# Row-maximum products of a pooled attention kernel moved onto 64 contraction rows each

## Chip, cores and metric

The kernel runs on one core of one Trainium2 chip, in one launch. The metric is the device time in microseconds; the time of before is the median of three runs.

## What is computed

```python
B, H, S, D = 4, 8, 1152, 64
q_pool = q.reshape(B, H, S // 2, 2, D).mean(axis=3)
scores = scale * np.matmul(q_pool, k.transpose(0, 1, 3, 2))
scores = scores - np.max(scores, axis=-1, keepdims=True)
attn = np.exp(scores)
attn = attn / (np.sum(attn, axis=-1, keepdims=True) + 1e-09)
x = np.matmul(attn, v)                  # heads joined: 2304 tokens of 512
# then top-2 of 8 experts: logits + softplus(x @ w_noise) * noise,
# out = sum over two experts of weight * relu(x @ w1[e]) @ w2[e], hidden 1024
```

The row maximum only shifts the exponent; the quotient is the same for any shift near it.

## The kernel before

Attention goes over 16 pairs. A pair is one head of two batches: 9 chunks of 128 pooled queries (chunks 0 to 3 of the first batch, 5 to 8 of the second, and chunk 4 half of each) against 9 key chunks of 128 for each batch. Float32 inputs are split into a high and a low float16 half. The transposed keys `kt` hold the high halves on partitions 0 to 63 and the low halves on 64 to 127; the transposed queries `qt` hold the high half twice, on both partition halves, so that one product over 128 contraction rows gives q_hi times (k_hi + k_lo). `score` (L342, L343) makes the scores, the second product bringing in the low half of the queries and the maximum (66 rows); `exp` (L350) is on ScalarE; `p_lo` (L355 on VectorE, L358 on GpSimd) makes the low half of the exponentials; `pv` (L378) multiplies with the values in 9 or 12 short products for each key chunk.

The row maximum comes ahead of the scores. `k_df` (L291, VectorE) writes `kd`, the difference of key chunks 0 to 3 and 4 to 7. For each query chunk, `max_mm` issues two products of 512 columns at L297: D = q times kd and S = q times key chunks 4 to 7, into two PSUM banks. `max_relu` (L305, ScalarE) takes relu(D), and `max_red` (L311, VectorE) reduces relu(D) + S to a maximum; `max_rest` and `rest_red` (L320) do the last key chunk. For chunk 4 each product is two, whose outputs are on PSUM partitions 0 to 63 and 64 to 127. There are four single banks: one for the sums of `pv`, two for D and S, one for the rest.

The order of each engine's instructions is written ahead by a planner (`Plan.run`), a list scheduler in Python with a cost, a key and the buffers of each operation. It always picks the operation that can start first by its costs, and among those within `WIN = 0.25` us the smallest key. The order that it finds is fixed; on the chip engines wait for one another by semaphores, and each engine takes its instructions in that order. After attention come the routing to experts and the experts' products (L937, L958), which run over sorted tokens.

Of the kernel before, what the change touches and what calls it, by code (L numbers as in the profile page):

```python
# [19 lines left out]
P = 128  # L20
# [4 lines left out]
NK = 9  # L25
D = 64
# [25 lines left out]
ND = 4  # L52
# [61 lines left out]
class Plan:  # L114
# [16 lines left out]
    def op(s, eng, cost, key, fn, deps=(), lat=None, port=False, take=(), give=(), ready=0.0, gen=None, after=None):  # L131
        o = Op(eng, cost, key, fn, lat, port, take, give)
        o.ready, o.gen = ready, gen
        s.hard += gen is None
        for tag in give:
            s.refs[tag] = s.refs.get(tag, 0) + 1
        for d in deps:
            if d.done is None:
                d.succ.append(o)
                o.wait += 1  # L140
            else:
                o.ready = max(o.ready, d.done)
        if after and after.done is None:
            after.then.append(o)
            o.wait += 1
        if not o.wait:
            s.can.append(o)
        return o
# [62 lines left out]
class Attn:  # L211
# [76 lines left out]

    def k_df(s, i, h):
        kt = s.G.buf["kt", i].rearrange("p (b c) t -> p b c t", b=2)  # L290
        s.nc.vector.tensor_sub(s.G.buf["kd", i][:, h], kt[:, h, 0:ND], kt[:, h, ND:2 * ND])  # L291

    def scores(s, i, ps, c, o, keys):
        parts = [(hh, slice(64 * hh, 64 * hh + 64)) for hh in range(2)] if c == 4 else [(int(c > 4), slice(0, P))]
        for hh, r in parts:
            m = keys(hh)
            s.nc.tensor.matmul(ps[r, o:o + m.shape[1] * P], s.G.buf["qt", i][:, c, r], m, start=True, stop=True)  # L297

    def max_mm(s, i, c):
        kt, kd = s.G.buf["kt", i], s.G.buf["kd", i]  # L300
        s.scores(i, s.G.buf["D", i, c], c, 0, lambda hh: kd[:, hh])
        s.scores(i, s.G.buf["S", i, c], c, 0, lambda hh: kt[:, hh * NK + ND:hh * NK + 2 * ND])

    def max_relu(s, i, c):
        s.nc.scalar.activation(s.G.buf["rd", i, c], s.G.buf["D", i, c], AF.Relu)  # L305
# [96 lines left out]
    def pairs(s):  # L402

        G = s.G
        op = G.op
# [5 lines left out]
        for i in range(NPAIR):  # L411
# [29 lines left out]
            qt, ql, a = [], [], None  # L441
            for p in ((0, 1) if x else (2,)):
                c = (slice(0, 3), slice(3, NCQ), slice(0, NCQ))[p]
                f = (c.stop - c.start) / NCQ
                a = op((("POOL", 0.1 + 1.45 * f), ("DVE", 0.07 + 0.74 * f)), 0, k(50, 92) + 8 * p * x,
                       lambda eng, i=i, c=c: (s.nc.vector if eng == "DVE" else s.nc.gpsimd).tensor_add(
                           B["qs", i][:, c], B["qr", i][:, c, 0], B["qr", i][:, c, 1]),
# [15 lines left out]
            for g in range(3):  # L463
                m = 3 * i + g
                k0 = 9 * m - 50 if x else b - 34 - ahead + 9 * g
                w = ((0,), (0, 1), (1,))[g]
                q = qt[min(g, len(qt) - 1)]
                red = []
                for ci in range(3):
                    c = 3 * g + ci  # L470
                    mm = op("PE", 0.62 if c == 4 else 0.43, k0 + 3 * ci, lambda i=i, c=c: s.max_mm(i, c),
                            deps=[df[h] for h in w] + [q],
                            take=[("bank", ("D", i, c)), ("bank", ("S", i, c))], give=[("kd", i)])
                    rl = op("ACT", 0.48, k0 + 3 * ci + 0.5, lambda i=i, c=c: s.max_relu(i, c), deps=[mm],
                            take=[("rd", ("rd", i, c))], give=[("D", i, c)])
                    red.append(op("DVE", 0.67, k0 + 3 * ci + 1, lambda i=i, c=c: s.max_red(i, c), deps=[rl],
                                  give=[("S", i, c), ("rd", i, c)]))
                rest = op("PE", 0.39 if g == 1 else 0.17, k0 + 5, lambda i=i, g=g: s.max_rest(i, g), deps=red, take=[("bank", ("R", i, g))])
                red.append(op("DVE", 0.47, k0 + 7, lambda i=i, g=g: s.rest_red(i, g), deps=[rest], give=[("R", i, g)]))
                allred += red  # L480
                if x or g == 2:
                    c = slice(3 * g, 3 * g + 3) if x else slice(0, NCQ)
                    fin = op("DVE", 0.6, k0 + 9, lambda i=i, c=c, g=g: s.max_fin(i, c, g), deps=allred + [ql[min(g, len(ql) - 1)]],
                             give=[("R", i, g)])
                    t = op("SP", 1.35, k0 + 9, lambda i=i, c=c: s.transpose(B["qt2", i][:, c], B["qn2", i][:, c]), deps=[fin],
                           lat=3.0, take=[("qt2", ("qt2", i))] if g == 0 or not x else (), give=[("qn2", i)], after=ready[0][0] if x and g else None)
                    for y in ((m,) if x else (m - 2, m - 1, m)):
                        ready[y] = [t] + [kc[h] for h in ((0,), (0, 1), (1,))[y % 3]]
# [17 lines left out]
        for n in range(NSEG):  # L506
            i = n // 3
# [6 lines left out]
            r = op("DVE", 0.65 + 0.1 * (n % 3 == 1), k1, lambda n=n: s.evac(n, 0), deps=done[-1:])  # L514
# [660 lines left out]
```

## Time and profile before

| what | value |
|---|---|
| runs | 893.82 us median of 3 (891.88 to 900.8) |
| profiled execution | 897.22 us |
| its span | 895.3 us |
| mean granted TensorE clock | 0.969 |
| TensorE matmul busy | 811.7 us |
| VectorE busy | 532.5 us |
| ScalarE busy | 444.2 us |
| GpSimd busy | 395.9 us |

The span runs from the first to the last instruction; the profiled execution has 1.9 us around it. Busy time is the union of an engine's instructions. A matmul's duration in the records is longer than the time from its start to the start of the next one, since matmuls overlap; the cost of one in a dense stretch is read from start to start.

### The profile page before, as it was taken

Reading aid. Unit: us, or ns where it says so; the run is one execution under the profiler, and the core shown is the slowest. Engines: PE = TensorE matmul, PEld = TensorE weight load, DVE = VectorE, ACT = ScalarE, POOL = GpSimd, SP = SyncE. Lnnn points to the kernel's source line nnn. Section 1 sums busy time; section 2 is a strip of 40 time slices with the busy share of each in tenths; the row PEclk is TensorE's granted clock in tenths of the full one; section 3 lists DMA queues with packets and bytes.
Section 4 is the critical chain, followed back from the end, with each engine's and each line's share of the span. In section 5 each row is a group of like instructions: output and inputs, shape, how many; then the busy total and the mean of one; then the engine's idle time right before and its main releaser. Section 6 shows DMA issues by size and latency. Waiting matters only on the chain.

```text
span 895.3 us, 21230 instructions
## 1 busy us (share of the span) xinstructions
PE 811.7 (91%) x8686; PEld 533.7 (60%) x8686; DVE 532.5 (59%) x1276; ACT 444.2 (50%) x663; POOL 395.9 (44%) x453
## 2 busy tenths in 40 slices
PE   3889999999989878799979499999999999999994
PEld 1547777777767746578846265756475655647442
DVE  4878898898889988999885042434233241422200
ACT  4758878777877655687523031333233232322310
POOL 4448889887984967763218202020201102020222
PEclk9989999999999979999989699999999999999998
DMA  8899796888899576657559916282827446291143
GB/s 194 163 247 248 159 230 176 196 200 190 187 223 202 122 192 185 146 166 151 104 168 351 131 32 147 82 213 71 218 66 201 83 131 153 72 223 14 24 56 41
DMA packets 213638, 137.81 MB, mean 154 GB/s; under 512 B 150304, under 2 KB 183584, under 8 KB 213536
## 3 DMA queue, kind: packets, MB, share of 16 engines
q1 hardware_dynamic: 204896, 116.33, 54.6%
q0 software_dynamic: 8640, 20.08, 11.1%
q8 instruction: 69, 1.13, 0.5%
q14 instruction: 33, 0.27, 0.1%
HBM read 62.14 MB, written 35.44 MB: 109 GB/s over the span
## 4 chain that ended last, share of the span: by engine, by line
PE 44%; POOL 2%; DMA 2%; DVE 1%; issue 1%; ACT 0%; POOLq 0%; ACTq 0%
PE pss L937 22%; PE psm L958 21%; POOL xg L99 1%; DMA xT<-xg 1%; PE psm L937 1%; POOL out_dram L99 0%; DMA xTg<-xr 0%; DVE wl L884 0%; PE psm L681 0%; ACT y L963 0%; DVE rt L730 0%; POOL sp L97 0%; DVE rt L748 0%; DVE hl L947 0%; DVE rt L710 0%
## 5 line engine op out<-in xcount | busy, mean ns | idle before, releaser
L358 POOL TENSOR_TENSOR pl<-pf 128x384 f16<-128x384 f32 x278 | 268.7, 996 | 101.6 <-ACT pf L350 90.6
L99 POOL DMA_INDIRECT out_dram<-y,mti x40 | 62.7, 1568 | 330.1 <-ACT y L963 318.8
L350 ACT ACTIVATE pf<-pss 128x768 f32<-128x768 f32 x216 | 173.6, 813 | 56.7 <-PE pss L343 50.0
L378 PEld LDWEIGHTS <-pf 128*128 128x128 bf16 x2880 | 157.8, 98 | 47.9 <-issue 18.2
L378 PE MATMUL psm<-vv,pf 128*128 128x65 f16 (+1 forms) x2880 | 168.2, 195 | 2.3 <-DVE kd L291 0.8
L378 PE MATMUL psm<-vv,pl 128*128 128x65 f16 (+1 forms) x1440 | 159.6, 194 | 2.7 <-POOL pl L358 1.8
L342 PE MATMUL pss<-qt,kt 128*128 128x384 f16 (+1 forms) x576 | 150.5, 290 | 4.1 <-ACT pf L350 3.9
L343 PE MATMUL pss<-qt,kt 66*128 66x384 f16 (+1 forms) x576 | 150.9, 291 | 0.0
L947 DVE SCALAR_TENSOR_TENSOR hl<-pss,hh 128x640 f16<-128x640 f32 (+2 forms) x68 | 50.2, 738 | 159.7 <-ACT hh L946 159.7
L378 PEld LDWEIGHTS <-pl 128*128 128x128 f16 x1440 | 127.6, 100 | 3.3 <-POOL pl L358 2.2
L958 PE MATMUL psm<-wh,hl 128*128 128x512 f16 x320 | 122.0, 381 | 0.0
L958 PE MATMUL psm<-wh,hh 128*128 128x512 f16 x320 | 122.0, 381 | 0.0
L958 PE MATMUL psm<-wl,hh 128*128 128x512 f16 x320 | 121.9, 381 | 0.0
L946 ACT ACTIVATE hh<-pss 128x640 f16<-128x640 f32 (+2 forms) x68 | 43.2, 636 | 137.7 <-PE pss L937 137.0
L311 DVE CUSTOM_DVE_ANT_0 rd<-psm,rd 128x512 f32<-128x512 f32 x144 | 97.3, 683 | 22.0 <-ACT rd L305 19.8
L958 PEld LDWEIGHTS <-hh 128*128 128x128 f16 x640 | 62.8, 98 | 74.2 <-issue 1.4
L963 ACT ACTIVATE y<-psm,mg 128x512 f32<-128x512 f32 x40 | 27.5, 688 | 157.4 <-issue 77.3
L305 ACT ACTIVATE rd<-psm 128x512 f32<-128x512 f32 x144 | 86.1, 598 | 25.2 <-PE psm L297 20.4
L297 PE MATMUL psm<-kt,qt 128*128 128x512 f16 (+3 forms) x320 | 79.5, 324 | 19.5 <-DVE mx L311 5.7
L937 PE MATMUL pss<-xT,fh 128*128 128x320 f16 (+1 forms) x448 | 85.4, 308 | 12.7 <-DMA xT<-xg 12.7
L355 DVE TENSOR_TENSOR pl<-pf 128x768 f16<-128x768 f32 x77 | 88.3, 1160 | 0.0
L937 PE MATMUL pss<-xT,wh 128*128 128x320 f16 (+1 forms) x448 | 83.5, 303 | 0.0
(158 smaller groups left out, 1162.1 us busy)
## 6 DMA issues: line engine op xcount, KB each, us to landing
xg<-zt SPq DMA_DIRECT2D x40, 260.0 KB
kr<-in_k_dram SPq DMA_DIRECT2D x32, 288.0 KB
vr<-in_v_dram SPq DMA_DIRECT2D x16, 576.0 KB
kr<-in_moe_w_dram SPq DMA_DIRECT2D x17, 512.0 KB
qr<-in_moe_w_dram SPq DMA_DIRECT2D x16, 512.0 KB
kn<-in_moe_w_dram SPq DMA_DIRECT2D x16, 512.0 KB
qr<-in_q_dram SPq DMA_DIRECT2D x31, 256.0 KB
vr<-in_moe_w_dram SPq DMA_DIRECT2D x15, 512.0 KB
```

The lines of the kernel that those rows point to most:

```text
L99: i = nc.gpsimd.indirect_dma_start(out=out, out_offset=bass.IndirectOffsetOnAxis(ap=idx, axis=0), in_=src, in_offset=None, **kw)
L297: s.nc.tensor.matmul(ps[r, o:o + m.shape[1] * P], s.G.buf["qt", i][:, c, r], m, start=True, stop=True)
L305: s.nc.scalar.activation(s.G.buf["rd", i, c], s.G.buf["D", i, c], AF.Relu)
L311: s.nc.vector.tensor_tensor_reduce(out=rd, in0=s.G.buf["S", i, c], in1=rd, scale=1.0, scalar=-3.0e38, op0=ALU.add, op1=ALU.max, accum_out= ...
L342: mm(ps[:, a, o:o + w], kt[:, hh * NK + kc, :], qf[:, q0:q0 + w], start=True, stop=False)
L343: mm(ps[:, a, o:o + w], kt2[0:66, hh * NK + kc, :], qf2[0:66, q0:q0 + w], start=False, stop=True)
L350: s.nc.scalar.activation(s.parts(u)[0], s.G.buf["ps", u][:, :, 0:SG], AF.Exp, scale=0.125 / (IN_SCALE * IN_SCALE))
L355: s.nc.vector.tensor_sub(pl, pf, ph)
L358: s.nc.gpsimd.tensor_sub(pl[:, a], pf[:, a], ph[:, a])
L378: mm(o[:, 0:x], src[:, t % 2, ci * P:ci * P + P], vv[:, hh * NK + kc, a:a + x], start=st, stop=last and src is pl, skip_group_check=True)
L937: nc.tensor.matmul(ps[:, i, 0:N], w[:, dc, f * P:(f + 1) * P], xT[:, 2 * dc + x, i * N:(i + 1) * N], start=(n == 0), stop=(n == 11))
L958: nc.tensor.matmul(ps, h[:, f, b * P:(b + 1) * P], w[:, f, :], start=(n == 0), stop=(n == 23))
```

## The change

The difference `kd` is made of the high key halves alone and written to partitions 64 to 127 of its tile, read from partitions 0 to 63 of `kt`. D is then a product over contraction rows 64 to 127 (the second copy of the queries' high half), and S one over rows 0 to 63 (the first copy, and the high key halves). The low key halves no longer enter D and S; `max_rest` is as before. The planner's cost of a pair goes from 0.43 to 0.26 us, and for chunk 4 from 0.62 to 0.34 us.

```diff
--- before.py
+++ after.py
@@ -288,18 +288,18 @@
 
     def k_df(s, i, h):
         kt = s.G.buf["kt", i].rearrange("p (b c) t -> p b c t", b=2)
-        s.nc.vector.tensor_sub(s.G.buf["kd", i][:, h], kt[:, h, 0:ND], kt[:, h, ND:2 * ND])
-
-    def scores(s, i, ps, c, o, keys):
+        s.nc.vector.tensor_sub(s.G.buf["kd", i][D:P, h], kt[0:D, h, 0:ND], kt[0:D, h, ND:2 * ND])
+
+    def scores(s, i, ps, c, o, keys, rows=slice(0, P)):
         parts = [(hh, slice(64 * hh, 64 * hh + 64)) for hh in range(2)] if c == 4 else [(int(c > 4), slice(0, P))]
         for hh, r in parts:
             m = keys(hh)
-            s.nc.tensor.matmul(ps[r, o:o + m.shape[1] * P], s.G.buf["qt", i][:, c, r], m, start=True, stop=True)
+            s.nc.tensor.matmul(ps[r, o:o + m.shape[1] * P], s.G.buf["qt", i][rows, c, r], m, start=True, stop=True)
 
     def max_mm(s, i, c):
         kt, kd = s.G.buf["kt", i], s.G.buf["kd", i]
-        s.scores(i, s.G.buf["D", i, c], c, 0, lambda hh: kd[:, hh])
-        s.scores(i, s.G.buf["S", i, c], c, 0, lambda hh: kt[:, hh * NK + ND:hh * NK + 2 * ND])
+        s.scores(i, s.G.buf["D", i, c], c, 0, lambda hh: kd[D:P, hh], slice(D, P))
+        s.scores(i, s.G.buf["S", i, c], c, 0, lambda hh: kt[0:D, hh * NK + ND:hh * NK + 2 * ND], slice(0, D))
 
     def max_relu(s, i, c):
         s.nc.scalar.activation(s.G.buf["rd", i, c], s.G.buf["D", i, c], AF.Relu)
@@ -468,7 +468,7 @@
                 red = []
                 for ci in range(3):
                     c = 3 * g + ci
-                    mm = op("PE", 0.62 if c == 4 else 0.43, k0 + 3 * ci, lambda i=i, c=c: s.max_mm(i, c),
+                    mm = op("PE", 0.34 if c == 4 else 0.26, k0 + 3 * ci, lambda i=i, c=c: s.max_mm(i, c),
                             deps=[df[h] for h in w] + [q],
                             take=[("bank", ("D", i, c)), ("bank", ("S", i, c))], give=[("kd", i)])
                     rl = op("ACT", 0.48, k0 + 3 * ci + 0.5, lambda i=i, c=c: s.max_relu(i, c), deps=[mm],
```

## Rows read from the trace of the kernel before

**Rows 1.** Windows of the span by stage, with busy time of each engine.
```profile
core 0: us, PE busy (x) PEld busy (x) DVE busy (x) ACT busy (x) POOL busy (x), PEclk, DMA share, GB/s
...
20.00:70.00 50.00, 42.10 (x439) 24.05 (x438) 42.15 (x99) 33.36 (x52) 24.57 (x23) 0.90 0.98 210
70.00:290.00 220.00, 208.93 (x3488) 158.86 (x3485) 196.49 (x446) 174.03 (x272) 178.08 (x181) 1.00 0.91 200
290.00:440.00 150.00, 130.08 (x2146) 100.78 (x2145) 137.75 (x316) 96.02 (x144) 98.52 (x119) 0.94 0.64 153
440.00:507.00 67.00, 47.77 (x401) 31.41 (x399) 37.22 (x219) 20.64 (x36) 25.80 (x41) 0.89 0.82 214
507.00:895.00 388.00, 376.85 (x2208) 216.74 (x2207) 110.88 (x178) 111.84 (x148) 60.54 (x75) 0.98 0.46 108
```

**Rows 2.** Chain that ended last, in order of time: start us, us, what.
```profile
438.76 0.39 PE psm L378 x7
...
494.20 12.87 DMA xT<-xg
```

**Rows 3.** Waits of TensorE, 70 to 290 us: in total, times, longest.
```profile
PE psm L297 <- DVE mx L311: 5.3, 7, 1.1
```

**Rows 4.** TensorE groups by form, 70 to 290 us: busy, mean ns, idle before.
```profile
L297 PE MATMUL psm<-kd,qt 128*128 128x512 f16 x76 | 28.8, 379 | 3.6 <-DVE mx L311 2.6 <-DVE qn L329 0.3 <-DVE ru L685 0.3
...
L297 PE MATMUL psm<-kd,qt 128*64 128x512 f16 x18 | 3.7, 402 | 1.2 <-DVE mx L320 1.2
```

**Rows 5.** Timeline of TensorE, an ordinary pair: start us, us, what.
```profile
200.34 0.33 PE L342 MATMUL pss<-qt,kt 128*128 128x384 f16 x1
200.50 0.33 PE L343 MATMUL pss<-qt,kt 66*128 66x384 f16 x1
200.66 0.38 PE L297 MATMUL psm<-kd,qt 128*128 128x512 f16 x1
200.88 0.38 PE L297 MATMUL psm<-kt,qt 128*128 128x512 f16 x1
201.10 0.22 PE L378 MATMUL psm<-vv,pf 128*128 128x65 f16 x2
```

**Rows 6.** The same timeline, a pair whose second product starts late.
```profile
201.83 0.38 PE L297 MATMUL psm<-kd,qt 128*128 128x512 f16 x1
202.29 0.38 PE L297 MATMUL psm<-kt,qt 128*128 128x512 f16 x1
202.51 0.32 PE L342 MATMUL pss<-qt,kt 128*128 128x384 f16 x1
```

**Rows 7.** Timeline of TensorE at the lower granted clock (0.50).
```profile
35.61 0.63 PE L297 MATMUL psm<-kd,qt 128*128 128x512 f16 x1
36.03 0.63 PE L297 MATMUL psm<-kt,qt 128*128 128x512 f16 x1
```

**Rows 8.** Timeline of TensorE, a middle chunk in two column halves.
```profile
171.39 0.25 PE L342 MATMUL pss<-qt,kt 128*128 128x192 f16 x1
171.47 0.25 PE L343 MATMUL pss<-qt,kt 66*128 66x192 f16 x1
171.65 0.41 PE L297 MATMUL psm<-kd,qt 128*64 128x512 f16 x2
171.89 0.38 PE L297 MATMUL psm<-kt,qt 128*64 128x512 f16 x2
172.21 0.23 PE L378 MATMUL psm<-vv,pf 128*128 128x65 f16 x2
```

**Rows 9.** The tile kd, 70 to 290 us: min, median, max ns.
```profile
L291 DVE TENSOR_TENSOR kd<-kt x19: 411/997/1069, 71.1 to 277.7; 128x512 f16<-128x512 f16 x19
```

**Rows 10.** Waits of ScalarE, 70 to 290 us.
```profile
ACT pf L350 <- PE pss L343: 23.8, 48, 1.1
...
ACT rd L305 <- PE psm L297: 2.7, 7, 0.6
```

**Rows 11.** Waits of TensorE, 290 to 440 us.
```profile
PE pss L342 <- ACT pf L350: 2.5, 2, 1.7
```

## Prediction

> **What bounds the kernel now.** I read the windows by stage first [rows 1]. From 507 us to the end TensorE is busy 376.85 of 388 us with the experts; nothing of the change is there. Attention lies between about 20 and 440 us. From 70 to 290 us TensorE is busy 208.93 of 220 us (95%) and VectorE 196.49 (89%), GpSimd 178.08 (81%), ScalarE 174.03 (79%). From 290 to 440 us VectorE has 137.75 of 150 us (92%), since the routing of the first half runs on it too, and TensorE 130.08 (87%). From 20 to 70 us no engine is over 85% and the DMA share is 0.98. So attention has no single bound: TensorE leads in the middle stage by six points over VectorE, and VectorE leads after it.
>
> The chain that ended last comes second. It has the last products with the values at 438.76 us, goes on through the routing, and holds a transposed load of 12.87 us from 494.20 us on [rows 2]; from there TensorE is all but always busy [rows 1]. Every microsecond by which attention ends earlier moves that chain, whose later pieces keep their lengths. The waits come third: in the middle stage TensorE stands for banks that VectorE has to release (5.3 us in 7 waits, [rows 3]), next to which its wait for data is small. The D products there are 76 of ordinary pairs and 9 of middle chunks (the row of 18 is two halves each), [rows 4], and S has as many; over the whole kernel there are 128 and 16.
>
> **The change, part by part.** *The streaming that is removed.* In an ordinary pair D starts at 200.66, S at 200.88 and the next product at 201.10 us [rows 5]: 0.22 us each, 0.44 a pair. The products ahead follow one another in 0.16 us, and D comes 0.16 us after the last, so neither entry nor exit costs anything today. If D and S run side by side, one 0.22 goes. That holds for the pairs whose S starts within 0.23 us of D: I counted 82 of the 128 (61 between 70 and 290 us, 15 from 290 to 440, 6 before 70). In 25 pairs S starts 0.44 us or more after D, as at 201.83 and 202.29 us [rows 6]: S waits, and streaming D beside it wins nothing. Of the 21 in between some 13 run at the lower clock, where a product takes 0.42 to 0.43 us [rows 7].
>
> *The switch that is added.* A 64-row product is another shape of the array than the 128-row products on either side. The trace has no such product; nearest are the middle chunks, which use the array in two column halves [rows 8]. There the last full product starts at 171.47 and would let the next start 0.085 us later (the spacing of its 192 columns), at 171.555; the halves start at 171.65: 0.095 lost on entry. The two halves run together (0.41 us for both, 0.40 for one, [rows 4, 8]). D to S takes 0.24, not 0.22. From S to the next full product, 171.89 to 172.21, are 0.32 where streaming needs 0.22: 0.10 lost on exit. At the other end are the 66-row products: those start 0.16 us after a full one like any other [rows 5], a price of nothing. So a switch there and back costs between 0 and 0.20 us. I take 0.20: the column halves show an array that is split in two and put together again, which 64 rows do too, while 66 rows still need its whole height. By the Trainium skill, "TensorEngine Tiling (Array Packing)", Tiling Modes, Key Properties, changing the tiling mode, and not only the tile, drains TensorE; the entry and exit of the column halves agree, and no run so far shows it for row halves.
>
> *The sum on TensorE.* An ordinary pair then takes 0.095 + 0.22 + 0.10 = 0.415 instead of 0.435 us (two times 0.2175): 82 times -0.02 is -1.6 us. The 25 pairs whose S waits keep that wait and gain an exit: 25 times +0.10 = +2.5. The 13 at the lower clock lose a streaming of 0.43 and gain 0.39, an estimate with entry and exit doubled as the streaming is: -0.5. I put the other 8 at nothing. A middle chunk already pays the switch, so one of its two rounds goes: 16 times -0.24 = -3.8. Together -3.4 us, where the planner's new costs would give 128 times 0.17 + 16 times 0.28 = 26.2.
>
> *VectorE.* `k_df` reads and writes half the partitions with the same 512 elements each. It takes 411 ns at best and 997 in the median here [rows 9]; I see no reason for either to change, and bound it by these: 32 instructions times -0.59 to +0.59 us if all fell to one end, -19 to +19 us of busy time, of which VectorE's idle time in the stage (23.5 of 220 us, [rows 1]) would hide a loss. I take 0. It is not moved past anything; its readers are the D products alone.
>
> *The order.* With other costs the planner writes another order for all engines, DMA issues too. If a pair really takes 0.415 us, the plan is 0.155 short for it. Each `max_relu` then stands in ScalarE's queue earlier than D can be there, with exponentials behind it, and so does each `max_red` in VectorE's. ScalarE now waits 2.7 us for D in the middle stage [rows 10] and has 46 us idle [rows 1], so I expect most of this to be covered; the rest is the slow rival's.
>
> *What reaches the end.* Of -3.4 us on TensorE I count half, since it leads in the stage that has most of it, but VectorE is six points behind there and ahead later: -1.7, or -2 rounded. The profiled execution goes from 897.22 to 895.2 us, and the median, 3.4 below it, from 893.82 to 892 us.
>
> **The rivals.** *The switch is nearly free.* For it speak the 66-row rows; against it the column halves. Then TensorE saves 82 x 0.22 = 18, 13 x 0.43 = 5.6 and 3.8: 27 us. In the middle stage that is 61 x 0.22 + 9 x 0.24 = 15.6, which takes TensorE's busy time from 209 to 193 us, under VectorE's 196.5; so VectorE becomes the bound and I count half, 8 us. From 290 to 440 us VectorE leads already: of some 5, 1. Before 70 us, half of 4, with DMA busy beside it. That is -11, at 883 us. By the same page, Overview, Theoretical Speedup, a contraction of 64 rows or fewer gains up to twofold from row tiling; by that rule alone the products' own time would halve, as this rival has it.
>
> *The order is written for a pair that the chip doesn't run (slower).* 144 pairs times 0.155 is 22 us by which the plan is ahead of TensorE over attention. Its place is ScalarE's queue: a `max_relu` that waits for D holds back an exponential, and the score products behind it find no free wide bank. TensorE waits 2.5 us for that from 290 to 440 us [rows 11]; in the middle stage it is ScalarE that waits for scores, 23.8 us [rows 10], which speaks against. It decides once ScalarE's waits for D exceed what it now waits for scores. Half of 22 reaching the end gives 905 us.
>
> *The halves don't run side by side.* If S starts 0.22 us after D all the same, the switch is pure cost, 82 x 0.20 = 16 us and 2.5 for the late ones, half of it on the path: 902 us; with a free switch, 894. Against it speaks that two column halves start together [rows 8].
>
> **How the numbers follow.** I give the forecast 0.55, the free switch 0.25, the order 0.12, halves in turn 0.08. A reordered plan alone may move the end by some microseconds either way, so the forecast's own range is 884 to 901, with 0.17 of it faster by over 1% (under 885) and 0.13 slower by over 1% (over 903); 1% is about what a measurement of this kernel can tell from no change, its runs being 9 us apart. Of the free switch 0.6 are faster by over 1% and the rest within, of the order rival 0.85 are slower, of the halves in turn half. Faster: 0.55 x 0.17 + 0.25 x 0.6 = 0.24. Slower: 0.55 x 0.13 + 0.12 x 0.85 + 0.04 = 0.21. Same: 0.55. The range must reach the middles of the first two rivals: 879 to 905.
>
> **What would show it.** In the timeline of the changed kernel, D and S of a pair start within 0.03 us of each other where banks are free (right), or 0.22 apart (third rival). The first product after the pair starts 0.32 us after S (switch as with columns) or 0.22 (free); D starts 0.09 later than the product ahead allows, or not. A middle chunk's four products start together and take 0.65 - 0.24 = 0.41 us in all. ScalarE's wait for D grows from 2.7 us in the middle stage if the order is the trouble, and TensorE's for ScalarE with it. The prediction is wrong if the exit is under 0.25 us, if VectorE's share passes 93% in the middle stage (then the free switch is real and VectorE binds), or if the windows from 440 us on change length.

## The result, and the profile after

The changed kernel takes 909.17 us (median of 4 runs, 907.48 to 911.21); before, run beside it, 896.91 us (median of 4). The ratio is 1.0123, with a 95% interval of 1.0084 to 1.0161. A run that is more than 1.5% above the fastest of its kernel is left out of the ratios and means below. The profiled execution has 911.21 us, a span of 909.4 and a mean granted clock of 0.956 (before: 897.22, 895.3, 0.969). It was forecast at 892, with 905 as the upper end.

The windows by stage, as in [rows 1]:

```profile
20.00:70.00 50.00, 37.98 (x404) 20.90 (x401) 41.42 (x97) 30.08 (x47) 20.31 (x19) 0.82 0.93 213
70.00:290.00 220.00, 210.22 (x3387) 148.37 (x3386) 193.30 (x431) 172.32 (x267) 170.96 (x175) 0.98 0.84 189
290.00:440.00 150.00, 126.26 (x2046) 94.17 (x2045) 133.84 (x315) 98.62 (x149) 103.76 (x121) 0.92 0.66 164
440.00:507.00 67.00, 52.60 (x603) 37.60 (x601) 46.54 (x230) 23.23 (x40) 27.29 (x42) 0.94 0.64 198
507.00:909.00 402.00, 385.09 (x2235) 219.86 (x2235) 112.45 (x187) 113.48 (x151) 64.11 (x79) 0.98 0.49 109
```

From 70 to 290 us the two kernels are alike: TensorE 210.22 (208.93), VectorE 193.30 (196.49). What differs stands ahead of that: from 20 to 70 us TensorE is busy 37.98 instead of 42.10 us, GpSimd 20.31 instead of 24.57, and the granted clock is 0.82 instead of 0.90. The chain of waits, as in [rows 2]:

```profile
450.46 0.39 PE psm L378 x7
...
508.79 12.72 DMA xT<-xg
```

The last products with the values start at 450.46 us, 11.7 later than before, so 11.7 of the 14.1 us of span are lost within attention. Most of the rest lies between them and the transposed load (58.33 instead of 55.44 us), a stretch whose length the prediction had as fixed. The starts of the exponentials (L350) in the trace date the loss: the 17th starts at 75.6 us (before 68.3), the 25th at 88.9 (81.1), the 137th at 291.3 (285.0), the last at 447.1 (435.9). Some 7 to 8 us are gone by 90 us, nothing more by 291, and the rest goes while the routing runs beside attention.

TensorE's timeline at an ordinary pair, to be read against [rows 5]:

```profile
202.61 0.25 PE L342 MATMUL pss<-qt,kt 128*128 128x192 f16 x1
202.69 0.25 PE L343 MATMUL pss<-qt,kt 66*128 66x192 f16 x1
202.87 0.39 PE L297 MATMUL psm<-kd,qt 64*128 64x512 f16 x1
202.87 0.39 PE L297 MATMUL psm<-kt,qt 64*128 64x512 f16 x1
203.19 0.24 PE L378 MATMUL psm<-vv,pf 128*128 128x65 f16 x2
```

D and S start together (3 ns apart), so they do run side by side. A score product of 192 columns starts 0.085 us after the one ahead; D starts 0.178 after it, 0.093 later than it could (0.095 in the median of 53 pairs). From S to the product behind are 0.32 us, 0.10 more than the streaming. A middle chunk, against [rows 8]:

```profile
204.26 0.25 PE L342 MATMUL pss<-qt,kt 128*128 128x192 f16 x1
204.35 0.25 PE L343 MATMUL pss<-qt,kt 66*128 66x192 f16 x1
204.53 0.40 PE L297 MATMUL psm<-kd,qt 64*64 64x512 f16 x2
204.53 0.40 PE L297 MATMUL psm<-kt,qt 64*64 64x512 f16 x2
204.87 0.24 PE L378 MATMUL psm<-vv,pf 128*128 128x65 f16 x2
```

Its four products start within 0.01 us and the next one follows 0.34 later. At the lower granted clock a pair looks like this (against [rows 7]):

```profile
74.99 0.52 PE L343 MATMUL pss<-qt,kt 66*128 66x384 f16 x1
75.45 0.60 PE L297 MATMUL psm<-kd,qt 64*128 64x512 f16 x1
75.45 0.61 PE L297 MATMUL psm<-kt,qt 64*128 64x512 f16 x1
75.99 0.29 PE L378 MATMUL psm<-vv,pf 128*128 128x65 f16 x2
```

Here D starts 0.46 us after a score product that needs 0.32 (the one ahead of it, at 74.67 us, took that), and the next product starts 0.54 after S, which needs 0.43 [rows 7]: 0.14 on entry and 0.11 on exit. In the middle stage the D products have this form:

```profile
L297 PE MATMUL psm<-kd,qt 64*128 64x512 f16 x73 | 28.6, 391 | 1.9 <-DVE mx L311 1.5 <-DVE kd L291 0.2
```

ScalarE's waits there, against [rows 10], and VectorE's difference, against [rows 9]:

```profile
ACT pf L350 <- PE pss L343: 28.9, 52, 3.3
ACT rd L305 <- PE psm L297: 5.1, 12, 0.8
```

```profile
L291 DVE TENSOR_TENSOR kd<-kt x17: 419/699/1037, 96.2 to 287.2; 64x512 f16<-64x512 f16 x17
```

ScalarE waits 5.1 instead of 2.7 us for D. The difference takes 699 ns in the median, within the old bounds. TensorE's waits from 290 to 440 us, against [rows 11]:

```profile
PE psm L378 <- DVE mx L311: 7.7, 2, 7.5
...
PE pss L342 <- ACT pf L350: 0.4, 1, 0.4
```

Its wait for ScalarE's exponentials has gone from 2.5 to 0.4 us; a single one of 7.5 us for a row maximum on VectorE is new, beside the routing. It is this one, in the timelines of TensorE and VectorE:

```profile
318.62 0.27 PE L378 MATMUL psm<-vv,pf 128*128 128x65 f16 x2 [7.47 <-DVE mx L311]
```

```profile
317.72 0.23 DVE L737 TENSOR_TENSOR rt<-rt,nz 128x72 f32<-128x72 f32 x1
317.87 0.68 DVE L311 CUSTOM_DVE_ANT_0 rd<-psm,rd 128x512 f32<-128x512 f32 x1
```

VectorE is at the routing alone (`rt`) from 300.28 to 317.87 us, and the reduction that frees a bank for the product with the values stands behind it.

### The profile page after: what moved, and what is told of

The parts are those of the page before. It is cut to its first block, busy times and chain, and to the rows that moved or that the text cites. A ratio compares the mean times of both kernels' runs of the same rounds, so it can differ in the third digit from the quotient of the medians.

```text
span 909.4 us, 21229 instructions
## 1 busy us (share of the span) xinstructions
PE 816.8 (90%) x8686; PEld 522.2 (57%) x8686; DVE 535.8 (59%) x1277; ACT 445.6 (49%) x663; POOL 394.8 (43%) x450
## 5 line engine op out<-in xcount | busy, mean ns | idle before, releaser
L358 POOL TENSOR_TENSOR pl<-pf 128x384 f16<-128x384 f32 x274 | 265.4, 998 | 108.9 <-ACT pf L350 96.4
L350 ACT ACTIVATE pf<-pss 128x768 f32<-128x768 f32 x216 | 173.7, 812 | 74.2 <-PE pss L343 57.4
L378 PEld LDWEIGHTS <-pf 128*128 128x128 bf16 x2880 | 151.4, 99 | 55.7 <-issue 45.6
L305 ACT ACTIVATE rd<-psm 128x512 f32<-128x512 f32 x144 | 85.6, 596 | 39.2 <-PE psm L297 31.4
L355 DVE TENSOR_TENSOR pl<-pf 128x768 f16<-128x768 f32 x79 | 92.5, 1188 | 1.3 <-ACT pf L350 1.0
L297 PE MATMUL psm<-kt,qt 64*128 64x512 f16 (+3 forms) x320 | 81.2, 332 | 12.9 <-DVE mx L311 6.2
```

The source lines that it names most:

```text
L350: s.nc.scalar.activation(s.parts(u)[0], s.G.buf["ps", u][:, :, 0:SG], AF.Exp, scale=0.125 / (IN_SCALE * IN_SCALE))
L355: s.nc.vector.tensor_sub(pl, pf, ph)
L358: s.nc.gpsimd.tensor_sub(pl[:, a], pf[:, a], ph[:, a])
L378: mm(o[:, 0:x], src[:, t % 2, ci * P:ci * P + P], vv[:, hh * NK + kc, a:a + x], start=st, stop=last and src is pl, skip_group_check=True)
```

## The experiments

Two theories stood against each other at first: A, that the order written by the new costs loses the time, and B, that the split products do. All ratios are to before, run beside each kernel; the five groups were measured on chips 3, 2, 2, 1 and 7 of the machine, each beside its own runs of before, whose mean went from 896.8 us in the first to 902.3 in the last. So kernels of one group are compared first. "Order of before" means that every engine has the instructions of before in the same order.

**First group: products and order apart.** e1_old_costs has the new products with the old costs, e2_new_costs the reverse:

```diff
-                    mm = op("PE", 0.34 if c == 4 else 0.26, ...      # e1: from the changed kernel
+                    mm = op("PE", 0.62 if c == 4 else 0.43, ...
-                    mm = op("PE", 0.62 if c == 4 else 0.43, ...      # e2: from the kernel before
+                    mm = op("PE", 0.34 if c == 4 else 0.26, ...
```

> The changed products with the planner's old costs (0.43 and 0.62), so that every engine has the order of before to the instruction. Theory A (the order written by the new costs is what costs; the products themselves save next to nothing): 0 to 4 us under before, ratio 0.995 to 1.0. Theory B (the split products cost time on the chip, by the switch or by the clock): slower by 8 to 14 us as the change is, ratio 1.009 to 1.016.

> The products of before (128 rows) in the order of the change: only the planner's two costs are changed to 0.26 and 0.34. Theory A (order): slower like the change or a little more, ratio 1.010 to 1.020, with some 7 us of it lost by the 16th exponential (75 us). Theory B (products): no slower than before, ratio within 0.004 of 1.

Measured: e1 907.43 us, 1.0116 (1.0033 to 1.0199); e2 905.71 us, 1.0106 (1.0005 to 1.0207). Both theories hold in part: either half of the change alone costs about as much as both together, though the order's interval only just clears 1. With the order alone (e2) the 25th exponential starts 4.5 us later than before, the 137th 2.0 and the last 9.9, so most of the order's loss falls beside the routing. TensorE's long wait for VectorE is there too (290 to 440 us in e2):

```profile
PE psm L378 <- DVE mx L311: 9.6, 3, 6.9
```

So that wait came with the order. It isn't peculiar to this order: the longest wait for VectorE in this stage is 3.2 us in before, 4.7 in e1 and 6.0 in e11, which have the order of before. Two more asked what in the order costs. e3_true_costs has `op("PE", 0.43, ...)` for every pair, the cost that the trace of the changed kernel shows; e4_fill_old has the old costs for `i < 3` and the new ones after.

> The changed products with what the trace of the changed kernel shows as their cost: 0.43 us for an ordinary pair and 0.43 for a middle chunk. Theory A1 (an order hurts because its costs are too low): with true costs the loss is gone, ratio 0.992 to 1.002. Theory A2 (any other order moves the time by about 1%, whether its costs are right or not): anywhere between 0.99 and 1.015, and not nearer to before than to the change.

> The changed products; old costs for the first three pairs of heads, new costs from the fourth on. If the loss sits in the fill before 75 us, as the first comparison of the traces has it (7.4 of 11.1 us by the 16th exponential): the 16th exponential is within 1 us of before and the total 2 to 6 us over before, ratio 1.002 to 1.007. If too low costs hurt everywhere: ratio 1.008 or more, with a loss that grows from pair to pair.

Measured: e3 897.29 us, 1.0013 (0.9972 to 1.0054); e4 907.31 us, 1.0109 (1.0028 to 1.0189), though its 17th exponential starts at 69.9 us, close to before. The loss isn't tied to the fill: in e4 it comes later. But e4 has the split products too, which lose as much in the order of before (e1), so it doesn't tell what its order adds.

**Second group: what the split products pay for.** For B there were now two explanations, L, entry and exit of the split array, and C, a granted clock that falls when fewer rows work. e5_old_products_true_costs is the kernel before with 0.43 for every pair (a third order). e6_late_only has the split products for `i >= 3` alone. e7_same_half keeps the switch and gives up running side by side; e8_column_halves keeps 128 rows and splits every product by columns:

```diff
-        s.nc.vector.tensor_sub(s.G.buf["kd", i][D:P, h], kt[0:D, h, 0:ND], ...)        # e7, costs as before
+        s.nc.vector.tensor_sub(s.G.buf["kd", i][0:D, h], kt[0:D, h, 0:ND], ...)
-        s.scores(i, s.G.buf["D", i, c], c, 0, lambda hh: kd[D:P, hh], slice(D, P))
+        s.scores(i, s.G.buf["D", i, c], c, 0, lambda hh: kd[0:D, hh], slice(0, D))
-        parts = [(hh, slice(64 * hh, 64 * hh + 64)) for hh in range(2)] if c == 4 else ...   # e8, D and S only
+        parts = [(hh if c == 4 else int(c > 4), slice(64 * hh, 64 * hh + 64)) for hh in range(2)] if c == 4 or split else ...
```

> The products of before (128 rows) in the order that 0.43 and 0.43 us give, the order of e3_true_costs to the instruction. Theory P (the split products cost some 4 to 9 us in any order, as they did in the order of before and in that of the change): 888 to 894 us where before has 898, ratio 0.988 to 0.996, and so faster than before. Theory Q (what the split products cost hangs on the order, and in this one it is nothing): like e3_true_costs, ratio 0.997 to 1.005.

> Order of before. The first three pairs of heads keep the 128-row products, the others have the split ones. If the split products lose their time in the fill (5.7 of the 11.5 us by the 20th exponential, near 75 us): the 20th exponential within 1.5 us of before, and the total 2 to 6 us over it, ratio 1.002 to 1.007. If the loss comes from the switch all along: ratio 1.008 or more.

> Order of before. D and S are both 64-row products over rows 0 to 63 (the difference is written to the lower half), so they keep the switch and run one after the other: a pair takes some 0.095 + 0.43 + 0.11 = 0.63 us where it takes 0.43. Half of the array streams at a time. Expected slower than the change's products in this order by half of 82 x 0.2 to all of it, 8 to 16 us: 915 to 924. Theory C (the granted clock falls with the part of the array that streams): its clock is under that of e8_column_halves by 0.005 or more, and its time over by 4 us or more. Theory L (what costs is the wait of entry and exit): the two are alike within 0.004.

> Order and arithmetic of before, but every product of D and S is made as two column halves that run side by side, as the middle chunks already are: the same switch, two rounds of streaming (some 0.65 us a pair), all 128 rows streaming. Theory L: like e7_same_half, 915 to 926 us. Theory C: its clock stays near 0.97 and it is faster than e7_same_half by 4 us or more.

Measured: e5 893.11 us, 0.9953 (0.9917 to 0.999); e6 903.99 us, 1.0081 (1.0042 to 1.0119); e7 908.74 us, 1.012 (1.0064 to 1.0175); e8 910.93 us, 1.0135 (1.0067 to 1.0203). A pair of e7 in TensorE's timeline:

```profile
205.09 0.25 PE L342 MATMUL pss<-qt,kt 128*128 128x192 f16 x1
205.18 0.25 PE L343 MATMUL pss<-qt,kt 66*128 66x192 f16 x1
205.36 0.39 PE L297 MATMUL psm<-kd,qt 64*128 64x512 f16 x1
205.58 0.38 PE L297 MATMUL psm<-kt,qt 64*128 64x512 f16 x1
205.89 0.24 PE L378 MATMUL psm<-vv,pf 128*128 128x65 f16 x2
```

Entry and exit are those of the changed kernel, but S starts 0.22 us after D. That makes some 0.2 us more for each pair than in e1, and the kernel is no slower than e1 by any difference that these runs can tell (908.74 and 907.43, in neighbouring groups). Side by side or not made no difference to the end in this order.

**Third group: switch or rows.** e9_fill_only is the complement of e6. e10_middle_only keeps 128 rows for ordinary pairs (with zeros on rows 0 to 63 of the difference, so that its high part alone counts in D) and splits the middle chunks alone, in the order of e5. e11_66_rows gives up the split but halves the rows at work: D and S leave out the low key halves but for two rows of them. e12_low_costs is the kernel before with 0.36 and 0.52 us as costs.

```diff
-        s.scores(i, s.G.buf["D", i, c], c, 0, lambda hh: kd[:, hh])                           # e11, from before
+        s.scores(i, s.G.buf["D", i, c], c, 0, lambda hh: kd[0:66, hh], slice(0, 66))
-        s.scores(i, s.G.buf["S", i, c], c, 0, lambda hh: kt[:, hh * NK + ND:hh * NK + 2 * ND])
+        s.scores(i, s.G.buf["S", i, c], c, 0, lambda hh: kt[0:66, hh * NK + ND:hh * NK + 2 * ND], slice(0, 66))
```

> Order of before. Only the first three pairs of heads have the split products, the complement of e6_late_only, which was 6 us over before. If the losses add up (e1_old_costs was 9 over): 2 to 5 us over before, ratio 1.002 to 1.006, with the loss in place by the 24th exponential and none after. If the fill loses nothing by the split: ratio within 0.002 of 1.

> Order of e5_old_products_true_costs. Ordinary pairs use 128 rows (rows 0 to 63 of the difference are zeros, so its high part alone counts in D), middle chunks alone the split products, where the switch is paid already. Theory L (only the switch costs, and streaming time on TensorE buys next to nothing): like e5_old_products_true_costs or up to 2 us under it, 890 to 894, ratio 0.991 to 0.997. If saved streaming counted in full: 3.8 us under it, 889.

> Order of before. D and S are each one product over contraction rows 0 to 65 (the high key halves and two rows of the low ones): about half of the arithmetic, but the form of the 66-row score products, which follows a 128-row one without a pause. Theory L (what costs is entry and exit of the split array): as before, ratio 0.996 to 1.004, D 0.22 us ahead of S. Theory C (fewer rows at work hold the clock down, and that costs): slower by over 4 us and a clock of 0.955 to 0.962 instead of 0.97.

> Products of before; the planner's costs are lowered to 0.36 and 0.52, about a third of the way to those of the change (which gave ratio 1.0106 with these products). Theory A1 (too low costs lose time in proportion): ratio 1.002 to 1.006. Theory A2 (each order is a draw of its own): anywhere from 0.992 to 1.015.

Measured: e9 902.8 us, 1.004 (1.0002 to 1.0078), so that e6 and e9 add up to e1; e10 892.86 us, 0.9922 (0.9875 to 0.9969); e11 901.4 us in the mean (before: 898.6), 1.0025 (0.9977 to 1.0073), with a clock of 0.963 in the mean of its runs against 0.968 for before; e12 911.24 us, 1.0101 (1.0064 to 1.0137). Costs lowered by about a sixth thus lose about as much as those of the change. A pair of e11:

```profile
201.30 0.25 PE L342 MATMUL pss<-qt,kt 128*128 128x192 f16 x1
201.39 0.25 PE L343 MATMUL pss<-qt,kt 66*128 66x192 f16 x1
201.47 0.38 PE L297 MATMUL psm<-kd,qt 66*128 66x512 f16 x1
201.69 0.38 PE L297 MATMUL psm<-kt,qt 66*128 66x512 f16 x1
201.90 0.23 PE L378 MATMUL psm<-vv,pf 128*128 128x65 f16 x2
```

66 rows enter and leave without a pause, as the 66-row score products do, and yet the clock is under that of before. Whether that costs time the interval of e11, which takes in 1, doesn't tell.

**Fourth group: the same three in the third order, and costs that are too high.** e14, e15 and e16 are e7, e8 and e11 with 0.43 for every pair; e13_high_costs is the kernel before with 0.50 and 0.72.

> Order of e5_old_products_true_costs (0.995 of before with 128-row products; 0.999 to 1.001 with the split ones). D and S both on rows 0 to 63, one after the other: switch, half the rows, no concurrency. If running D and S side by side is worth nothing to the end: like e3_true_costs, ratio 0.996 to 1.005. If it is worth its 0.2 us a pair: 8 to 16 us more, ratio 1.008 or more.

> Same order; all of D and S in column halves with 128 rows: switch, all rows at work. Theory L (entry and exit cost): 4 us or more over e5_old_products_true_costs, ratio 0.999 to 1.006, clock near 0.967. Theory C (rows at work, by the clock): within 2 us of e5_old_products_true_costs, ratio 0.993 to 0.998.

> Same order; D and S over 66 rows: no switch, about half the rows at work. Theory L: like e5_old_products_true_costs, ratio 0.993 to 0.998, clock 0.967 or more. Theory C: 3 to 6 us over it, ratio 0.999 to 1.003, clock 0.962 or less.

> Products of before; costs raised to 0.50 and 0.72, over what the trace shows. Theory A1 (too low costs lose time, in proportion): no slower than before, ratio 0.99 to 1.002. Theory A2 (each order is a draw of its own, whatever its costs): 0.992 to 1.015, and a ratio over 1.004 or a gain over 0.99 would both speak for it.

Measured: e14 910.6 us, 1.0098 (1.0071 to 1.0125); e15 905.26 us, 1.0064 (1.0032 to 1.0095); e16 897.36 us, 0.9941 (0.9918 to 0.9965); e13 907.65 us, 1.004 (1.0007 to 1.0072). With about the same rows at work (66 and 64) and D and S one after the other in both, the switch takes e16 to e14: 1.6%, 13 us. The clock is 0.9625 in e16, 0.959 in e14, 0.967 in e15, where all rows work. But it is 0.960 in e13, which has the 128-row products in another order: the order moves the clock about as much as the rows do.

**Fifth group: does the lower clock cost time?** e5 and e16 once more, side by side.

> The kernel of e5_old_products_true_costs once more, beside the next one on the same chip. Ratio 0.992 to 0.998, clock 0.967 to 0.971.

> The kernel of e16_66_rows_o3 once more, in the same order as the one before it, with about half the rows at work and no switch. If the lower clock (0.962 against 0.969) costs time: 3 to 7 us over the one before it. If its time at the lower clock falls where TensorE has to wait anyway: within 2 us of it.

Measured: e17 889.23 us, 0.9855 (0.982 to 0.9891), clock 0.970; e18 897.35 us, 0.9949 (0.9924 to 0.9974), clock 0.960. No run of e17 is over 892.2 and none of e18 under 894.05: 8 us. The ratios of the same two kernels in the earlier groups, 0.9953 and 0.9941, show no such difference. The windows show where the clock differs; first e17, then e18 (columns as in [rows 1]):

```profile
55.00:60.00 5.00, 2.46 (x23) 1.14 (x23) 4.83 (x11) 1.98 (x4) 1.61 (x2) 0.96 1.20 224
60.00:65.00 5.00, 4.63 (x15) 1.61 (x15) 4.18 (x12) 1.49 (x3) 0.17 (x1) 0.50 1.20 199
65.00:70.00 5.00, 5.00 (x35) 2.59 (x32) 3.24 (x7) 4.11 (x7) 2.83 (x3) 0.86 0.97 308
70.00:75.00 5.00, 4.75 (x83) 3.96 (x80) 4.80 (x12) 4.72 (x9) 4.34 (x4) 1.00 1.11 255
75.00:80.00 5.00, 5.00 (x93) 4.12 (x92) 4.38 (x15) 5.00 (x9) 3.94 (x5) 1.00 1.00 251
```

```profile
55.00:60.00 5.00, 2.46 (x22) 1.01 (x21) 4.97 (x9) 1.68 (x4) 0.59 (x1) 0.95 1.19 209
60.00:65.00 5.00, 4.89 (x17) 1.84 (x16) 3.72 (x10) 2.34 (x4) 1.10 (x1) 0.50 1.18 218
65.00:70.00 5.00, 5.00 (x19) 2.19 (x18) 1.99 (x4) 2.87 (x4) 1.91 (x3) 0.50 1.02 338
70.00:75.00 5.00, 5.00 (x66) 3.96 (x64) 4.32 (x11) 3.11 (x6) 2.42 (x3) 0.69 1.16 232
75.00:80.00 5.00, 5.00 (x83) 4.08 (x80) 3.23 (x8) 4.90 (x9) 3.39 (x4) 1.00 0.35 105
```

Both fall to 0.50 after TensorE stood half of the stretch from 55 to 60 us (busy 2.46 of 5 us in both), while the row maxima of the third pair of heads are made. From 65 to 70 us TensorE is busy all the time in both, and e17 has 0.86 back, e18 still 0.50; e18 reaches the full clock only after 70. e1, with the split products, stays at half for longer still:

```profile
65.00:70.00 5.00, 5.00 (x17) 1.61 (x15) 2.31 (x6) 2.51 (x4) 2.97 (x3) 0.50 1.01 298
70.00:75.00 5.00, 5.00 (x36) 2.69 (x35) 3.60 (x7) 3.75 (x7) 2.46 (x3) 0.50 1.11 252
```

## Why the prediction was wrong, point by point

**Right: the pair on TensorE.** Forecast 0.095 + 0.22 + 0.10 = 0.415 us; the trace has 0.093 + 0.22 + 0.10. At the lower clock the forecast doubled entry and exit to 0.39; they took 0.25. The switch costs with rows what it costs with columns, and D and S run side by side. The rule of the Trainium skill, "TensorEngine Tiling (Array Packing)", Tiling Modes, Key Properties, that a change of the tiling mode drains TensorE, agrees with these rows; its Theoretical Speedup (Overview) of up to twofold is not what a lone pair between full products gets here.

**Wrong: the sum on TensorE left the granted clock out.** I added up TensorE's time between 20 and 440 us from the starts in the trace: against the spacing that each form has in a dense stretch at the full clock (0.216 us for 512 columns, 0.163 for 384, 0.085 for 192, 0.030 for 65), what is over goes to the half clock where a product's duration shows it, to short gaps (0.02 to 0.16 us, above all the switch), or to waits over 0.16 us. Each row is one profiled execution; that of e11 took 907.45 us, 6 over the mean of its runs.

| kernel | half clock | short gaps | waits |
|---|---|---|---|
| before | 13.4 | 7.4 | 51.2 |
| the changed kernel | 17.4 | 27.8 | 57.9 |
| e2: 128 rows, order of the change | 16.8 | 8.3 | 55.3 |
| e1: split products, order of before | 22.2 | 28.8 | 52.4 |
| e11: 66 rows, same order as e1 | 21.3 | 7.4 | 51.7 |
| e7: same half, same order | 21.5 | 28.3 | 31.2 |
| e8: column halves, same order | 15.4 | 30.3 | 37.2 |
| e17: 128 rows, third order | 12.2 | 8.6 | 46.1 |
| e18: 66 rows, third order | 21.3 | 8.4 | 40.3 |
| e3: split products, third order | 19.1 | 29.1 | 44.5 |

From before to the changed kernel the switch adds 20.4 us, the half clock 4.0 and waits 6.7. The last exponential comes 11.2 later, so the streaming saved is the rest, 31.1 - 11.2 = 19.9 us. Switch and streaming nearly cancel (+0.5, where I had -3.4): that step held. Two terms that the prediction put at nothing make the loss, and they are the steps that failed: the half clock, which its sum didn't have since it took the prices of a full clock for the whole stage, and the waits, of which the order alone brings 4.1 (e2, below).

From before to e1, with the order kept, the switch adds 21.4 us, the half clock 8.8 and waits 1.2; the streaming saved is 31.4 - 11.5 = 19.9. There the clock is most of the loss. In these two orders, that of before and the third, the kernels with about half the rows at work in all of D and S (e1, e3, e7, e11, e14, e16, e18) have 19 to 22 us of it, those with all rows (before, e5, e8, e10, e15, e17) 10 to 15, whatever their gaps. 128-row products in other orders have 16.8 to 17.8 (e2, e12, e13), so the order has its part in it. How much of the 4.0 us is the order's isn't shown: the profiled execution of e2 has the lowest clock of its four (0.959), and in the mean of the runs the clock is 0.970 in before, 0.964 in e2, 0.958 in e1 and 0.957 in the changed kernel.

What the clock costs in time isn't settled. 66 rows against 128 took 8 us more in the fifth group and 2.9 in the mean of the third; the fourth group against the second, between which before moved by 4 us, shows nothing. In the profiled executions e18 has 9.1 us more of half clock than e17 but 5.8 less of waits, and its last exponential comes 3.1 us later. Runs of one kernel differ in clock as well: over 91 runs of before, each against the mean of its group, a clock lower by 0.01 goes with 3.7 us more, over 137 runs of the other kernels with 4.8; which of the two brings the other isn't shown.

**Wrong: "of -3.4 us on TensorE I count half".** TensorE's lead in busy time was no bound. e7 streams some 0.2 us a pair more than e1, and its waits over 0.16 us shrink from 52.4 to 31.2: TensorE had that time to give. By the order of the operations S isn't awaited for as long as the relu of D (598 ns in the mean, L305) runs, so an earlier S doesn't help the row maximum, while D, on which it hangs, comes 0.1 us later, by the entry; no run takes this chain apart. In the order of before, streaming that is taken away behind D came back as waiting. It isn't nothing in every order: e14 has 1.0098 and e3, of another group, 1.0013.

**Wrong: "I expect most of this to be covered".** The order alone costs 1.06% (e2), and with it TensorE's waits grow by 4.1 us. That was my slow rival, but not its mechanism: TensorE's wait for ScalarE, its place, shrank from 2.5 to 0.4 us, and the long wait is one for VectorE beside the routing. That its 905 us lies near the 905.71 of e2 is luck. The loss also doesn't follow how far the costs are off. Costs lowered by a sixth lose 1.01%, by 40 to 45% 1.06%, costs too high 0.4%; and the costs of e5, which charge a middle chunk 0.43 us where it takes 0.65 [rows 8], gain 0.5 to 1.5%. The theory that too low costs lose in proportion (A1) falls; the orders tried with the 128-row products came out between 1.5% under before and 1.1% over it, and their costs don't tell which is good. What in an order makes it good stays open. Order and products don't add up either (1.06 and 1.16, together 1.23%), and no run shows why; the clocks above don't add up in the same way.

**The other rivals.** A nearly free switch is refuted by the timelines, halves that run in turn as well. The expected sign of the first, VectorE over 93% in the middle stage, isn't there (193.30 of 220). Two smaller workings were off without weight: half of 16 and 2.5 us over 893.82 gives 903 for halves in turn, not 902, and the rows bound the difference on VectorE at 1069 ns, which is 0.07 over its median and not 0.59.

**A faster kernel.** The 128-row products in the third order (e5 and e17, 0.9953 and 0.9855) beat both kernels, and so does e10 (0.9922), which splits where the switch is paid already. What e10 adds to e5 lies within what groups differ by.

## What to carry to other kernels

Splitting the array pays by what streams between one switch and the next: at 0.2 us for there and back, a lone pair of 512 columns just breaks even, so collect several pairs behind one switch, or split only what is split already. Ask of streaming that is saved who waits for its end; where a chain hangs on the first product, perhaps nobody waits for the second. Where a planner writes the order, run the new products in the old order and the old products in the new one before either is blamed, for the order alone can move the time by as much as the edit.

## What I had not expected

With order and streaming unchanged, products that use 66 of 128 rows ran at a lower granted clock: 0.960 against 0.970 in the mean of the runs of e18 and e17, 0.963 against 0.968 for e11 and before. The fall itself comes after TensorE stood, in either profiled execution; with half the rows it stayed at 1.2 GHz for some 6 us longer although TensorE was busy throughout. The same kernel against the same reference came out at 0.9953 (chip 2) and 0.9855 (chip 7) in two groups, with intervals that don't meet, so one group's interval understates what two groups can differ by. Whether the chip makes it isn't shown.
